# Raw pieces of the query and key projections: the copy to the high part on ScalarE alone, with all tables made anew

## The chip, the cores and the metric

The kernel runs on one core of a Trainium2 chip. The metric is the device time of one execution in microseconds. Before the change it is 384.94 us, the median of three runs (384.48 to 385.16). The names of the engines in rows are PE (TensorE), PEld (its weight load), DVE (VectorE), ACT (ScalarE), POOL (GpSimd) and SP (SyncE, which here only issues DMAs).

## The reference

Attention inside chunks of 64 tokens, then a layer of four attention experts over its output, of which each token takes the best two:

```python
def _attn_ref(q, k, v):                       # B, H, S, D = 8, 8, 576, 64
    ...                                       # q_c, k_c, v_c: nine chunks of 64 tokens
    scores = scale * np.matmul(q_c, k_c.transpose(0, 1, 2, 4, 3))
    attn = softmax(scores)                    # exp, divided by the sum + 1e-09
    out = np.matmul(attn, v_c)

def _moe_ref(x, w_gate, wq, wk, wv, wo):      # x: 8 x 576 x 512, E = 4, Hd = 64, K = 2
    logits = x @ w_gate
    topk = np.argpartition(-logits, K, axis=-1)[..., :K]
    w = softmax(logits of the two chosen)
    for e in range(E):
        q, k, v = x @ wq[e], x @ wk[e], x @ wv[e]
        scores = where(causal, -1e9, scale * (q @ k.transpose(0, 2, 1)))
        a = softmax(scores)
        ye = a @ v @ wo[e]
        out += (w of e, if e was chosen) * ye
```

All of it is in fp32. The kernel keeps that precision by splitting a factor into a high part (rounded to the type fp32r) and a low part (what is left), and by adding three matmuls for one: high by high, low by high, high by low.

## The kernel before

The 8 x 576 tokens are 36 groups of 128. `stage_a` takes one or two groups through the chunk attention (matmuls at L437, softmax on DVE, ACT and POOL, turned weights, matmuls at L504) and leaves x, high and low, in a chunk of two or three groups. Per chunk there are four query/key projections (`project_qk`, matmuls at L549, 128 x 384 in the large chunks) and per group one projection of the values and the gate (`project_v`, L409). Per batch and pair of experts there are `scores` (L671, then mask and minimum on DVE at L682, exp on ACT at L694), `weights` (scaled on POOL at L716, turned by half-turns on PE at L334, by POOL's copy at L341 with a DMA and ACT's copy at L350, and by DVE at L751), `values` (L768) and, per batch, `project_out` (L796, then a copy and the store).

A chunk of 384 tokens can reach over the end of a batch of 576. Then `project_qk` makes two parts of it. The first goes from the PSUM bank straight to the high part and the low part of the batch's queries or keys. The second belongs to the next batch, whose buffer is not yet free. It goes from the bank to a raw buffer `zr` (L554, L556, L558), which frees the bank, and later in two steps from there: a copy of `zr` to the high part (`qh` or `kh`), and the subtraction `zr` minus high part into the low part (`ql` or `kl`, L588). There are 16 such raw pieces in the program, in the batches 1, 3, 5 and 7: four of 64 columns and twelve of 192.

Nothing is scheduled at run time. `Plan.add` lists the operations. Three tables, written out in the file, say the rest: `ORDER` is the order in which all operations are emitted, and with it each engine's queue, `HOMES` gives each tile its buffer, and `SIDES` says of each operation with an `alt` whether it takes its first engine (0) or the alternative (1). Among those are all copies out of PSUM banks (ACT or DVE), the subtractions (POOL or DVE) and, before the change, the copy of a raw piece:

```python
o1 = add("ACT", act_t(n, sbuf=True), lambda f=f: f(a_copy), deps=[o1], uses=[raw, z],
         alt=("DVE", dve_t(n), lambda f=f: f(dve.tensor_copy)))        # L584, L585; runs as L583
```

The entries `w412`, `w62` and so on in `ORDER` are warm-up matmuls without use (bank, then count), all in the first 20 us. An engine works its queue strictly in order; what stands behind a waiting instruction waits too.

Of the kernel before, what the change touches and what calls it, by code (L numbers as in the profile page):

```python
# [116 lines left out]
def dve_t(n):  # L117
    return 0.075 + 1.04e-3 * n


def act_t(n, aps=0, sbuf=False):
    return (0.093 if aps or sbuf else 0.052) + 0.833e-3 * n + 0.093 * aps
# [7 lines left out]
43 63 40 109 86 66 89 w412 69 25 70 72 20 w62 46 71 73 132 47 74 49 48 75 161 50 76 51 77 112 52 10 w615 92 53 5 54 28  # L130
93 155 23 95 29 94 w03 55 96 115 57 97 78 24 116 56 98 79 80 192 99 118 w74 81 100 117 119 84 82 158 120 85 w22 101 83
# [112 lines left out]
def chunked_attention_then_attention_experts(ctx: ExitStack, tc: tile.TileContext, qt, kt, vt, wqk, wvg, wo, out):  # L244
    nc = tc.nc
    pe, dve, act, pool = nc.tensor, nc.vector, nc.scalar, nc.gpsimd
    plan = Plan()
    add = plan.add
# [282 lines left out]
    def project_qk(c, m):  # L531
# [28 lines left out]
        for k, (b, s0, n, c0) in enumerate(parts):  # L560
            z = z_s[b, pair]
# [13 lines left out]
            else:  # L575
                raw = own[k]
# [297 lines left out]
```

## Time and profile before

| | |
|---|---|
| median of three runs | 384.94 us (384.48 to 385.16) |
| the profiled execution | 383.89 us |
| its span, first to last instruction | 382.2 us |
| PE busy | 367.4 us, 96% of the span |
| DVE, ACT, POOL busy | 315.3, 282.1, 270.1 us |
| mean granted TensorE clock | 0.994 |

A busy PE is a PE whose pipelined matmuls cover the time; their ends are modelled. The time between the span and the execution's own time, 1.7 us, lies around the program. The profile is of one execution, 1.05 us faster than the median.

### The profile page before, as it was taken

The numbers are of one execution on the slowest core, as the hardware profiler recorded it, in microseconds if no ns is written. First come the engines' busy times: TensorE is split into PE (matmuls) and PEld (weight loads), VectorE is DVE, ScalarE is ACT, GpSimd is POOL, SyncE is SP. The second block draws the span as 40 slices with busy tenths as digits, with TensorE's granted clock in tenths as the row PEclk, the third lists the DMA queues.
The fourth block names the chain that finished last, engine by engine and source line by source line (L and its number), as shares of the span: only waits on it lengthen the run. The fifth ranks groups of instructions, "written<-read, shape, count | busy, mean of one in ns | idle before, by whom it ended". The sixth has DMA issues, their size and how long they took to land.

```text
span 382.2 us, 12795 instructions
## 1 busy us (share of the span) xinstructions
PE 367.4 (96%) x4876; PEld 310.3 (81%) x4876; DVE 315.3 (83%) x1040; ACT 282.1 (74%) x675; POOL 270.1 (71%) x477
## 2 busy tenths in 40 slices
PE   7999999999999999679999999999999999998996
PEld 3599989888898898577988979988798799776765
DVE  2899799899996689989986998989989588777742
ACT  1564698899796997559696687968975879998450
POOL 5546589887988459488987248979795459989700
PEclk9999999999999999989999999999999999999999
DMA  7997777989898749766665777648488303365764
GB/s 269 392 338 216 148 194 181 205 155 204 212 239 152 164 151 173 205 194 117 176 123 140 155 190 198 100 138 165 129 113 154 68 3 61 59 134 96 169 204 165
DMA packets 114221, 63.49 MB, mean 166 GB/s; under 512 B 94576, under 2 KB 94832, under 8 KB 114160
## 3 DMA queue, kind: packets, MB, share of 16 engines
q1 hardware_dynamic: 114016, 62.42, 68.5%
q8 instruction: 38, 0.62, 0.7%
q10 hardware_dynamic: 144, 0.26, 0.2%
q14 instruction: 23, 0.19, 0.2%
HBM read 30.42 MB, written 9.44 MB: 104 GB/s over the span
## 4 chain that ended last, share of the span: by engine, by line
PE 67%; DVE 15%; POOL 6%; ACT 6%; DMA 3%; issue 2%; SPq 0%; ACTq 0%; POOLq 0%; DVEq 0%
PE bank L549 19%; PE bank L409 12%; PE bank L796 11%; PE bank L768 10%; PE bank L671 7%; PE bank L437 3%; PE bank L504 3%; PE bank L334 2%; DVE at L682 2%; POOL at L716 2%; DVE mx L454 2%; DVE xl L519 2%; ACT at L694 2%; DVE kh L583 2%; POOL wp L341 2%
## 5 line engine op out<-in xcount | busy, mean ns | idle before, releaser
L694 ACT ACTIVATE at<-at,st 128x320 f32<-128x320 f32 (+4 forms) x160 | 88.3, 554 | 18.1 <-DVE st L682 17.9
L716 POOL TENSOR_SCALAR at<-at,st,gate 64x64 f32<-64x64 f32 (+4 forms) x160 | 95.6, 609 | 7.8 <-DVE st L707 5.5
L350 ACT ACTIVATE aT<-wpT 128x768 uint16<-128x768 uint16 (+1 forms) x64 | 66.3, 1055 | 5.9 <-DMA wpT<-wp 5.8
L549 PE MATMUL bank<-xh,wqk_hi 128*128 128x384 f32 (+1 forms) x208 | 68.4, 336 | 2.3 <-DVE e L449 2.3
L682 DVE CUSTOM_DVE_ANT_0 at<-bank,mask 64x64 f32<-64x64 f32 (+4 forms) x160 | 61.1, 418 | 9.2 <-PE bank L671 8.9
L341 POOL COPY wp<-at 128x768 uint16<-128x768 uint16 (+1 forms) x64 | 58.4, 930 | 13.6 <-DMA wpT<-wp 13.4
L549 PE MATMUL bank<-xh,wqk_lo 128*128 128x384 f32 (+1 forms) x208 | 66.2, 326 | 0.0
L465 POOL TENSOR_TENSOR en<-e,mx 128x512 f32<-128x512 f32 x36 | 37.2, 1044 | 24.5 <-DVE mx L456 21.5
L768 PE MATMUL bank<-aT,vv 128*64 128x448 f32 (+4 forms) x384 | 47.2, 393 | 0.8 <-DVE e L449 0.7
L768 PEld LDWEIGHTS bank<-aT,vv 128*64 128x64 f32 x384 | 25.3, 137 | 22.7 <-issue 15.3
L549 PEld LDWEIGHTS bank<-xh,wqk_hi 128*128 128x128 f32 x208 | 39.4, 189 | 4.7 <-DVE e L449 2.5
L549 PE MATMUL bank<-xl,wqk_hi 128*128 128x384 f32 (+1 forms) x208 | 42.6, 326 | 0.0
L350 ACT ACTIVATE et<-wpT 128x1024 uint16<-128x1024 uint16 x31 | 35.9, 1174 | 6.7 <-DMA wpT<-wp 6.7
L549 PEld LDWEIGHTS bank<-xh,wqk_lo 128*128 128x128 f32 x208 | 39.6, 190 | 0.2
L409 PE MATMUL bank<-wvg_hi,xh 128*128 128x260 f32 x144 | 37.8, 294 | 0.0
L751 DVE STREAM_TRANSPOSE aT<-at 32x96 f32<-32x96 f32 x128 | 34.5, 269 | 3.4 <-PE bank L768 0.7
L409 PE MATMUL bank<-wvg_lo,xh 128*128 128x260 f32 x144 | 36.1, 283 | 0.0
L549 PEld LDWEIGHTS bank<-xl,wqk_hi 128*128 128x128 f32 x208 | 35.5, 191 | 0.0
L452 ACT ACTIVATE e<-e 128x1024 f32<-128x1024 f32 (+1 forms) x21 | 19.6, 935 | 20.7 <-DVE e L449 20.5
L341 POOL COPY wp<-en 128x1024 uint16<-128x1024 uint16 x31 | 32.3, 1057 | 3.2 <-DMA wpT<-wp 3.2
L671 PE MATMUL bank<-kh,qh 64*128 64x288 f32 (+4 forms) x192 | 32.1, 331 | 0.4 <-DVE st L682 0.3
L447 DVE TENSOR_REDUCE mx<-bank 128x8 f32<-128x512 f32 (+1 forms) x42 | 24.3, 603 | 8.5 <-PE bank L437 8.3
(112 smaller groups left out, 866.4 us busy)
## 6 DMA issues: line engine op xcount, KB each, us to landing
vs<-in_vt_dram SPq DMA_DIRECT2D x36, 256.0 KB, 4.5
ks<-in_kt_dram SPq DMA_DIRECT2D x36, 256.0 KB, 3.9
qs<-in_qt_dram SPq DMA_DIRECT2D x35, 256.0 KB, 4.4
out_dram<-y SPq DMA_DIRECT2D x35, 256.0 KB, 2.3
wpT<-wp SPq DMA_TRANSPOSE x95, 3.3
at<-in_wqk_dram SPq DMA_DIRECT2D x4, 256.0 KB, 6.0
at<-in_wvg_dram SPq DMA_DIRECT2D x2, 260.0 KB, 5.3
at<-in_wo_dram SPq DMA_DIRECT2D x2, 256.0 KB, 5.3
```

The costliest lines, as they stand in the source:

```text
L341: pool.tensor_copy(p.t[:, :256 * n].rearrange("p (x n) -> p x n", x=2), src().bitcast(U16).rearrange("p (n x) -> p x n", x=2))
L350: act.activation(put().bitcast(U16).rearrange("p j (q x) -> p j q x", x=2), pt.t[:, :256 * n].rearrange("p (x j q) -> p j q x", x=2, j=n), ...
L409: pe.matmul(bk.t[0:rows, :W_VG], xp[:, k, cols], wp[:, k, :], start=(n == 0), stop=(n == 3 * KT - 1))
L465: pool.tensor_tensor(en.t.rearrange("p (s h k) -> p s h k", s=2, h=HP), ev, rv.to_broadcast([128, 2, HP, 64]), op=OP.mult)
L549: pe.matmul(bk.t[:, :width], wp[:, k], xp[:, k, 0:width], start=(n == 0), stop=(n == 3 * KT - 1))
L671: pe.matmul(bks[s].t[:rows(i), at:at + c1 - c0], q[own, cs], k[own, c0:c1], start=(x == 0), stop=(x == 2), skip_group_check=True)
L682: dve.tensor_tensor_reduce(out=a.t[:r, A_OFF[i] + c0:A_OFF[i] + c1], in0=bk.t[:r, at:at + w], in1=mask[:r, m0:m0 + w], scale=1.0, scalar=f ...
L694: act.activation(af, af, AF.Exp, scale=-1.0, bias=st.t[:r, 0, i, 0:1], accum_out=st.t[:r, 1, i, 0:1])
L716: pool.tensor_scalar(af, af, st.t[:r, 2, i, 0:1], gt.t[:r, i, e:e + 1], op0=OP.mult, op1=OP.mult)
L751: dve.transpose(dst, src)
L768: pe.matmul(bk.t[64 * s:64 * s + 64, c0 - h0:h1 - h0], vs.t[:, j, 64 * (2 * pair + s):64 * (2 * pair + s) + 64], ts[s].t[:, 448 * j + c0:4 ...
L796: pe.matmul(bk.t[:, n0:n1], up[:, k, 128 * t:128 * t + 128], wp[:, k, n0:n1], start=(n == 0), stop=(n == 5), skip_group_check=True)
```

## The change

One line of Python loses its alternative, and the three tables are other tables. The copy of a raw piece is on ACT in all 16 cases; before, `SIDES` had 7 of them on ACT and 9 on DVE.

```diff
@@ project_qk
                 def f(copy, raw=raw, z=z, cs=cs, n=n):
                     copy(z.t[hi][:, cs], raw.t[:, 0:n])
-                o1 = add("ACT", act_t(n, sbuf=True), lambda f=f: f(a_copy), deps=[o1], uses=[raw, z],
-                         alt=("DVE", dve_t(n), lambda f=f: f(dve.tensor_copy)))
+                o1 = add("ACT", act_t(n, sbuf=True), lambda f=f: f(a_copy), deps=[o1], uses=[raw, z])
@@ ORDER (first line; all others differ too, and there is one line more)
-43 63 40 109 86 66 89 w412 69 25 70 72 20 w62 46 71 73 132 47 74 49 48 75 161 50 76 51 77 112 52 10 w615 92 53 5 54 28
+63 43 40 25 135 109 86 w49 69 70 72 66 71 73 20 w45 46 74 132 28 49 75 50 112 29 155 47 76 48 77 51 10 52 5 w616 78 53
...
@@ HOMES, SIDES: other digits throughout
```

Because `ORDER` is one text line longer, lines of the changed kernel above the edit have numbers one higher (L450 for L449, L312 for L311); from L586 on they are the same, since the edit takes one line away.

The multiset of the other instructions is the same but for sides. Of the copies out of PSUM, 18 of turned weights (`aT`) and 4 of `et` go from ACT to DVE; 8 of `uh`, 5 of `y` and 2 of `vv` go from DVE to ACT; among `xh`, `qh`, `kh` and `zr` some change places both ways. Of the subtractions of raw pieces 9 of 16 are on DVE in both. Of the eight subtractions of weights, DVE has one of `wqk` and two of `wo` before, and one of `wqk` and one of `wvg` after. The warm-up matmuls are 34 instead of 38.

On DVE, in the second half of the scores of batch 2 (experts 2 and 3), this is what stands around a raw piece of batch 3's keys before the change (`zr` is the raw piece, `kh` and `kl` its high and low part, `mx` and `e` the maximum and the exponents of the chunk attention; `ISA` is the masked minimum of L682):

```order
L519 TENSOR_TENSOR xl1_96<-bank2_63,xh1_94 128x2x128
L449 TENSOR_TENSOR e0_81<-bank0_61,mx2_91 128x8x64
L751 STREAM_TRANSPOSE aT0_115<-at1_112 32x3x32 x4
L583 CAST kh1_106<-zr0_97 128x192
L447 TENSOR_REDUCE mx2_91<-bank6_67 128x8
L588 TENSOR_TENSOR kl1_108<-zr0_97,kh1_106 128x192
L449 TENSOR_TENSOR e0_81<-bank6_67,mx2_91 128x8x64
L682 ISA at0_111,st0_123<-bank4_65,mask_145 128x288
```

On DVE the same piece (and its query twin) now leaves only the subtraction:

```order
L682 ISA at2_113,st1_124<-bank6_67,mask_145,st1_124 128x288
L682 ISA st1_124 128x1
L588 TENSOR_TENSOR ql0_103<-zr2_99,qh0_101 128x192
L801 COPY y0_127<-bank7_68 128x512
L682 ISA at0_111,st0_123<-bank5_66,mask_145 128x320
L682 ISA st0_123 128x1
L588 TENSOR_TENSOR kl0_107<-zr0_97,kh0_105 128x192
L801 COPY y2_129<-bank2_63 128x512
```

The cast is gone from DVE's queue, and the chunk attention's subtraction at L449 no longer stands behind one.

On ACT, these are the rows of the queue in the same stretch before the change, with no raw piece among them (`at` are the exps of the scores, `vv` and `y` copies out of banks):

```order
L694 ACTIVATE at2_113,st1_124<-at2_113,st1_124 128x448
L311 ACTIVATE y0_127<-bank5_66 128x512
L311 ACTIVATE y1_128<-bank1_62 128x512
L350 ACTIVATE aT1_116<-wpT2_122 128x3x256
L694 ACTIVATE at2_113,st1_124<-at2_113,st1_124 64x64
L311 ACTIVATE y2_129<-bank0_61 128x512
L452 ACTIVATE e0_81<-e0_81 128x16x64
```

On ACT the two pieces now stand between the exps of these scores:

```order
L453 ACTIVATE e0_81<-e0_81 128x16x64
L555 ACTIVATE kh1_106<-bank1_62 128x384
L312 ACTIVATE vv1_110<-bank3_64 64x260 x2
L694 ACTIVATE at0_111,st0_123<-at0_111,st0_123 128x192
L312 ACTIVATE qh0_101<-zr2_99 128x192
L312 ACTIVATE kh0_105<-zr0_97 128x192
L694 ACTIVATE at0_111,st0_123<-at0_111,st0_123 128x576
L694 ACTIVATE at2_113,st1_124<-at2_113,st1_124 128x192
```

Each of the two waits until PE has read the buffer that it writes, and the exps behind them wait with them.

At the start of the program SP issued its loads in this order (`ks` and `qs` are keys and queries of a group, `vs` its values, `at` here the landing place of weights):

```order
L327 DMA vs0_77<-in_vt_dram 128x512
L323 DMA ks0_73<-in_kt_dram 128x512
L324 DMA qs0_69<-in_qt_dram 128x512
L323 DMA ks1_74<-in_kt_dram 128x512
L323 DMA ks2_75<-in_kt_dram 128x512
```

Now it issues them so:

```order
L324 DMA ks0_73<-in_kt_dram 128x512
L325 DMA qs0_69<-in_qt_dram 128x512
L328 DMA vs0_77<-in_vt_dram 128x512
L324 DMA ks1_74<-in_kt_dram 128x512
L384 DMA at0_111<-in_wvg_dram 128x520
```

The first group's keys and queries come ahead of its neighbour's values, and half of the value weights comes ahead of the third group.

## Rows read from the trace of the kernel before

**Rows 1.** The page: busy time, share of the span and instructions of each engine.
```profile
PE 367.4 (96%) x4876; PEld 310.3 (81%) x4876; DVE 315.3 (83%) x1040; ACT 282.1 (74%) x675; POOL 270.1 (71%) x477
```

**Rows 2.** Timeline, PE: start, us, line, tiles, count, idle before and releaser.
```profile
156.74 0.44 PE L549 MATMUL bank<-xh,wqk_hi 128*128 128x384 f32 x1 [2.26 <-DVE e L449]
...
159.04 0.71 PE L334 MATMUL bank<-ident,at 64*128 64x64 f32 x16
...
160.62 1.09 PE L504 MATMUL bank<-et,vs 64*64 64x64 f32 x58 [0.60 <-DVE kl L573]
...
164.40 1.15 PE L437 MATMUL bank<-ks,qs 64*64 64x64 f32 x60 [2.61 <-DVE ql L570]
...
165.48 0.44 PE L549 MATMUL bank<-xh,wqk_hi 128*128 128x384 f32 x1
...
169.06 0.42 PE L409 MATMUL bank<-wvg_hi,xh 128*128 128x260 f32 x1
```

**Rows 3.** Timeline, DVE, the same stretch.
```profile
149.71 5.51 DVE L583 CAST kh<-zr 128x192 fp32r<-128x192 f32 x1
...
156.01 0.68 DVE L449 TENSOR_TENSOR e<-bank,mx 128x512 f32<-128x512 f32 x1
...
161.92 1.70 DVE L583 CAST qh<-zr 128x192 fp32r<-128x192 f32 x1
```

**Rows 4.** Timeline, POOL, the same stretch.
```profile
149.69 2.04 POOL L465 TENSOR_TENSOR en<-e,mx 128x512 f32<-128x512 f32 x2
151.73 1.42 POOL L716 TENSOR_SCALAR at<-at,st,gate 128x320 f32<-128x320 f32 x2
153.09 1.03 POOL L341 COPY wp<-en 128x1024 uint16<-128x1024 uint16 x1
154.07 1.04 POOL L341 COPY wp<-at 128x1024 uint16<-128x1024 uint16 x1
155.10 0.39 POOL L716 TENSOR_SCALAR at<-at,st,gate 64x64 f32<-64x64 f32 x1
160.84 3.07 POOL L716 TENSOR_SCALAR at<-at,st,gate 128x448 f32<-128x448 f32 x5 [5.35 <-DVE st L707]
```

**Rows 5.** Stretches: us, busy (x) of PE, PEld, DVE, ACT, POOL, granted clock, DMA.
```profile
166.00:169.40 3.40, 3.40 (x13) 3.40 (x12) 3.40 (x6) 0.92 (x3) 3.40 (x5) 0.50 0.80 270
```

**Rows 6.** Line L583: count, min/median/max ns, first and last start, forms.
```profile
L583 DVE CAST kh<-zr x6: 243/274/5514, 49.9 to 308.5; 128x192 fp32r<-128x192 f32 x5, 128x64 fp32r<-128x64 f32 x1
L583 DVE CAST qh<-zr x3: 177/306/1701, 53.0 to 161.9; 128x192 fp32r<-128x192 f32 x2, 128x64 fp32r<-128x64 f32 x1
```

**Rows 7.** Timeline, POOL and DVE, near 230 us.
```profile
229.11 2.16 POOL L341 COPY wp<-en 128x1024 uint16<-128x1024 uint16 x2
...
229.89 0.47 DVE L588 TENSOR_TENSOR ql<-zr,qh 128x192 fp32r<-128x192 f32 x1
230.28 1.09 DVE L583 CAST kh<-zr 128x192 fp32r<-128x192 f32 x1
```

**Rows 8.** Line L390, the subtractions of weights.
```profile
L390 DVE TENSOR_TENSOR wo_lo<-at,wo_hi x2: 678/1001/1324, 26.9 to 35.0; 128x512 fp32r<-128x512 f32 x2
```

**Rows 9.** Groups by shape, ACT: busy us, mean ns, idle before.
```profile
L311 ACT ACTIVATE qh<-zr 128x192 fp32r<-128x192 f32 x4 | 1.4, 361 | 0.0
```

**Rows 10.** Timeline, PE, near 349 us.
```profile
348.89 0.47 PE L334 MATMUL bank<-ident,at 64*128 64x64 f32 x8 [1.27 <-POOL at L716]
349.28 0.50 PE L796 MATMUL bank<-wo_hi,uh 128*128 128x512 f32 x1
349.62 0.40 PE L796 MATMUL bank<-wo_lo,uh 128*128 128x512 f32 x1
349.85 0.40 PE L796 MATMUL bank<-wo_hi,uh 128*128 128x512 f32 x1
```

**Rows 11.** Timeline, SP and PE, the first microseconds.
```profile
1.74 0.42 SPq L324 DMA_DIRECT2D qs<-in_qt_dram  x1
...
1.25 4.88 PE L834 MATMUL bank<-warm 128*128 128x512 bf16 x12 [1.25 <-DVE warm L281]
```

More of the change, by code (lines that the diff above doesn't have):

```diff
@@ L129 @@
 ORDER = """
-43 63 40 109 86 66 89 w412 69 25 70 72 20 w62 46 71 73 132 47 74 49 48 75 161 50 76 51 77 112 52 10 w615 92 53 5 54 28
-93 155 23 95 29 94 w03 55 96 115 57 97 78 24 116 56 98 79 80 192 99 118 w74 81 100 117 119 84 82 158 120 85 w22 101 83
[82 rows of a table removed]
+63 43 40 25 135 109 86 w49 69 70 72 66 71 73 20 w45 46 74 132 28 49 75 50 112 29 155 47 76 48 77 51 10 52 5 w616 78 53
+115 80 79 54 23 118 161 116 24 w32 92 119 117 81 95 120 93 55 84 96 89 56 121 82 57 192 94 122 58 83 97 123 85 98 0 59
+61 60 w52 138 13 99 62 124 100 139 158 8 757 141 198 140 14 142 125 15 143 126 101 35 758 144 9 127 102 30 103 167 128
[82 rows of a table added]
@@ L214 @@
 """
 HOMES = """
-2103110231111672300010100002345332450212765412230113033275002010010363633111004111211010063022200340020322100037100322
-0321311220211450111222671112110100671220113370010220311140012233013131110226700001112400101103002412200022502020011003
-5333112060202001122430221003431100221311711221003161301001222763300024311112202002603330016200100003115110021130702021
-2110171221000060003201201170332641310013070260710162140151143001057002112574201000057221173314212336342610122110200221
-4727002611124506472156510200217645031011113700220135611233751046102211422200064000526172505025042420630710310511300211
@@ L221 @@
-2335361520111000422002737710021734273010011122211760501705030651412411213327635401000224311110554730021462610102200031
-1221702415240512250040610201025103173311106233127651340122112400115107732100166521012020211201160540723031343440316112
-3334342501012021122036327300212124631012202512013003522050015171450451217017176006105301512331725421012125320012762650
-02124643001122053200101101162223264014471531332014017012001350112534753012074474701122053120112065040327111
+2103110231111457600020100004532332011313270312236702025061001140000764511022145111100021132033300262021322000002111033
@@ new lines @@
+3741302001111030002223731102121120351331000070000121301010031100413001013222501133322000002213107211110027402021211205
+2330221461100011322020111330450202011122611222111061300011322373302225311132200012102211134700020111106710022235602110
+0022117330001200001211012210112531303215300230511030673111563112014002167350201202064211215432032131537151020015112012
+1713122001167464376247012520012071460101016320124557531233621740100110150122202701701210011114007331616513206220300033
+3126134471001104010226743052100765264100122751010655342615032316631213733124251211001102610224123152100167260011001402
@@ L225 @@
+2222114221230715031040726314141107002204005713320573420122107011011463162100721630010221531200410401706211376252014513
+3210352701121234002156643601201704501000120300214243015221123001230756111374157067000205733126151200112000621002143460
+12010735201121202210071213022426137754561203312164302012112602100755776200105570601001260002112407161105230
 """
 SIDES = """
-0010001100010110000000000001000010110010000000111110100010001011000000111001100010111110011000001100100010100010001001
-1010111010010011110111001001100100100111011100100100111000110100100011111101111010010000111110011110000010111110110011
@@ L229 @@
-0111101001101010001001110100011011011010110101010111110000100011001101001101001101101000100110110011000001110010011011
-111101101111111101010111100
+0001010000000100010111011011000000110000110000100010111000101101001110000010111010111110100111111010011111101100100100
+1011111110001111111001111100110110101011000110110000001101100110000100110110101101000101110010001001110011001110001100
+1101111010100001011000101110011111111011011001001000110100001101101110111011101011110010110111110001111110011110111000
@@ L231 @@
+01000000000
 """
```

164 rows, old and new, of the table ORDER are left out of this document.

## The prediction

> **What bounds the kernel now.** I read the page's busy times first. TensorE is covered for 367.4 of 382.2 us [rows 1], so the time is its own work plus 14.8 us of idle time, and DVE, ACT and POOL matter only where TensorE waits for them. Then I read the waits of PE, and its timeline where they are long. Three of the waits lie within 10 us, at 156.74, 160.62 and 164.40: 2.26 + 0.60 + 2.61 = 5.47 us, all for DVE [rows 2]. The largest other wait behind the start is 1.27 us [rows 10]. The reader is to see that this one place is the only one of its size.
>
> The cause is on DVE in the same stretch: the copy of a raw piece, 128 x 192 out of SBUF into SBUF, starts at 149.71 and takes 5.51 us [rows 3]. The line's median is 274 ns [rows 6]. POOL works without a gap from 149.69 to 155.10 + 0.39 [rows 4], and DVE goes on just as that burst ends, at 155.22. A second copy takes 1.70 us at 161.92, inside a burst that starts at 160.84 and lasts 3.07 us [rows 3, 4]; a third takes 1.09 us at 230.28 and ends (231.37) when two POOL copies end (231.27) [rows 7]. The six others found no such burst. So a copy on DVE that reads and writes SBUF waits until POOL pauses. L449, two places behind the long copy, frees a bank for TensorE; it starts at 156.01, and TensorE starts at 156.74.
>
> A rule stands close to this. The Trainium skill's page "SBUF — State Buffer", section "Who interferes with whom", says that DVE in its two-port mode and GpSimd take a shared pair of ports as an exclusive lock, held for one whole instruction, and that the later one blocks until the first has finished. By that, the copy would wait for one POOL instruction, 1.04 us at most here [rows 4], which DVE could make good (3.0 us of slack, below), and the change would gain nothing at this place. The trace disagrees: one copy waited out a whole burst of seven instructions. I go by the rows.
>
> After the third wait the granted clock is 0.50 for 3.4 us [rows 5], the lower of the two levels, 1.2 GHz; TensorE had been idle for 5.47 of the 11 us before it fell.
>
> **The change part by part.**
>
> The nine copies leave DVE. The long one with its median of 0.27 us would end 5.24 us earlier, L449 would end at 156.01 + 0.68 − 5.24 = 151.45, and TensorE wants its bank at 156.74 − 2.26 = 154.48: it is 3.0 us early, and the first wait goes. The third wait is for the low part of the queries, which stands on DVE right behind the second held copy; with 1.43 and the backlog of 5.24 us gone it goes too. The 0.60 us are a wait for the low part of keys that TensorE itself had computed just before (bank out, high part, low part, bank free), and I leave them in. Gain 2.26 + 2.61 = 4.87 us; ends 2.26 (the first alone) and 5.47. What is late next at this place is that 0.60.
>
> The clock. Twelve matmuls of one projection took 169.06 − 165.48 = 3.58 us at the low level and 159.04 − 156.74 = 2.30 at the full one [rows 2]. Without the stall I count the difference as gained, 1.28 us; ends 0 (it falls elsewhere) and 1.28.
>
> The copies arrive on ACT: nine at 361 ns [rows 9] are 3.2 us, beside 100 us in which ACT is idle (382.2 − 282.1, [rows 1]). ScalarE's seven copies before the change include no long one (four of 192 columns have a mean of 361 ns, and no idle time before them). Cost 0, hidden by TensorE's own work; if that cover is missing, a copy costs what it takes, 3.2 us in all. The wait that it adds: nine of the sixteen wait for PE to have read the buffer they write, and behind them stand exps of the scores, which POOL and then TensorE wait for. That is a rival below.
>
> The other sides that change (18 and 4 copies to DVE, 15 to ACT) leave both engines under TensorE's load: DVE idles 67 us, ACT 100 [rows 1]. Cost 0; if a bank comes free late because of one, the price is a wait like the largest other one, 1.27 us [rows 10]. The nine subtractions on DVE stay nine.
>
> The written order. In the old order TensorE changes between its four shapes of matmul (128 x 128, 64 x 128, 128 x 64, 64 x 64) 141 times, in the new one 134 times, counted in the order of both. One change costs, at 349.28, the first step of 0.34 us instead of 0.23 [rows 10], so 0.11 us. Seven fewer are 0.8 us; ends 0 (hidden in a wait) and 0.8.
>
> The start. The first group's queries are issued one load earlier, 1.74 becoming some 1.3 us [rows 11], a gain of one issue, about 0.4. Against it DVE gets the low part of half the value weights as its ninth instruction, 0.68 us [rows 8], ahead of the chain that the first turned weights wait for, and it waits there for a load. The four warm-up matmuls less are 4 x 4.88 / 12 = 1.6 us at most [rows 11]; they fill time in which TensorE waits for loads, so I count nothing for them. The start is 0 in the sum; ends −2.0 and +0.7. In the end of the program both orders hold back the same thirteen output projections to fill the last two weight chains; 0.
>
> Sum: 4.87 + 1.28 + 0.8 = 7.0 us. The span becomes 375.2, the execution 376.9 with the 1.7 us around it. The profiled execution was 1.05 us below the median, so the median to expect is 377.9 us.
>
> **Rivals.**
>
> Slower: ACT's queue stops at the raw pieces. Five pairs of pieces of 192 columns now stand side by side in ACT's queue, each behind a wait for PE (the one shown for batch 3 among them), and each stops the exps behind it. For it: before, only two of seven on ACT waited for PE. Against it: the four in the row showed no idle time [rows 9]. Priced by the longest wait that TensorE showed, 2.61 us [rows 2], it outweighs the gain from three pairs on; with four it is 377.9 + 10.4 = 388.3 us. Chance 0.11.
>
> Given back: another order has other waits. For it: the order is new throughout, and a wait like the 0.60 us [rows 2] comes of order alone. Against it: the old order's largest wait of its own is 1.27 us [rows 10]. Three such waits make 381.7 us. Chance 0.16.
>
> The burst holds the subtractions instead. Two inputs in SBUF, on DVE, now beside the burst of POOL's weights in batch 2. For it: L390 took 1324 ns once instead of 678 [rows 8]. Against it: at 229.89 one of 192 columns took 0.47 us in the middle of POOL's copies, where the copy of the same width behind it took 1.09 us and waited for their end [rows 7]. The stall of 4.87 + 1.28 would be back: 384.1 us. Chance 0.05.
> The same page and section speak for this rival: an instruction of DVE with two SBUF inputs contends with a GpSimd instruction that reads SBUF. The trace agrees with some price (0.65 us at L390), not with a full block.
>
> The change doesn't remove what the median holds: the long copy was an accident of the profiled execution. Against it: that execution was the fastest shown (383.89 against 384.48 to 385.16). Time 384.1 us, chance 0.03.
>
> **How the numbers follow.** The forecast holds 0.65. Its own range: 2.3 to 5.5 for the stall, 0 to 1.3 for the clock, 0 to 0.8 for the shapes and −2.0 to +0.7 for the start, which do not all fall on one side, give 375 to 381 us. The range for 8 in 10 takes in the order's rival and the edge of the two at 384.1, and at the low end one more of the old waits gone and a good start: 373.5 to 384.0. A difference under 0.2%, 0.8 us, can't be told from none here. Faster than 384.2: 0.65, nearly all of 0.16 and 0.03 of the two cases at 384.1, so 0.83. Slower than 385.7: 0.11. The same: 0.06.
>
> **What the next profile would show.** No DVE instruction in its table that copies `zr`, and no DVE instruction outside the start far over its group's mean; PE's waits for `e` at L450 and `ql` at L571 of over 2 us gone; a mean clock near 1.0 with no fall before the end; sixteen copies of `zr` on ACT with means near 0.36 us. Wrong would be: a subtraction at L588 of over 1 us on DVE, ACT idle for PE at the raw copies, or new PE waits that sum to over 8 us behind the start.

## The result

The changed kernel takes 380.05 us (median of four, 378.66 to 380.55) beside 384.71 us for the kernel before (384.24 to 385.16): ratio 0.9873, 95% interval 0.9844 to 0.9902, a gain of 4.7 us where 7.0 were forecast. The profiled execution took 380.55 us, its span is 378.8. The two profiled executions, 383.89 and 380.55, lie 3.3 us apart, less than the medians; what is read from profiles below accounts for these two.

The page of the kernel after, busy times; the kernel before is in [rows 1]:
```profile
PE 364.5 (96%) x4872; PEld 309.4 (82%) x4872; DVE 312.4 (82%) x1043; ACT 285.7 (75%) x672; POOL 270.3 (71%) x477
```
TensorE's busy time fell by 2.9 us, its idle time from 14.8 to 378.8 − 364.5 = 14.3. That is odd for a change that was to take away waits of 4.87 us. The timeline of PE says why; three new waits stand there, 1.18 + 2.36 + 2.55 = 6.09 us, where [rows 2] had 5.47:
```profile
159.74 0.50 PE L796 MATMUL bank<-wo_hi,uh 128*128 128x512 f32 x1 [1.18 <-DVE ql L571]
...
163.76 0.59 PE L410 MATMUL bank<-wvg_hi,xh 128*128 128x260 f32 x1 [2.36 <-ACT aT L312]
...
321.62 0.39 PE L410 MATMUL bank<-wvg_hi,xh 128*128 128x260 f32 x1 [2.55 <-DVE kl L574]
```
The copies are as forecast: none on DVE, sixteen on ACT with medians of 348 ns ([rows 9] had a mean of 361). Line L312, count, min/median/max ns, first and last start:
```profile
L312 ACT ACTIVATE qh<-zr x8: 240/348/356, 45.1 to 311.6; 128x192 fp32r<-128x192 f32 x6, 128x64 fp32r<-128x64 f32 x2
L312 ACT ACTIVATE kh<-zr x8: 240/348/366, 52.3 to 311.3; 128x192 fp32r<-128x192 f32 x6, 128x64 fp32r<-128x64 f32 x2
```
But the instruction behind the copy, the subtraction at L588 that makes the low part, is now held in its place. Line L588 on DVE, first in the kernel before, then after:
```profile
L588 DVE TENSOR_TENSOR ql<-zr,qh x5: 227/343/469, 73.1 to 309.5; 128x192 fp32r<-128x192 f32 x4, 128x64 fp32r<-128x64 f32 x1
L588 DVE TENSOR_TENSOR kl<-zr,kh x4: 342/350/389, 137.7 to 309.2; 128x192 fp32r<-128x192 f32 x4
```
```profile
L588 DVE TENSOR_TENSOR ql<-zr,qh x5: 185/346/2354, 46.2 to 314.7; 128x192 fp32r<-128x192 f32 x3, 128x64 fp32r<-128x64 f32 x2
L588 DVE TENSOR_TENSOR kl<-zr,kh x5: 437/1011/3383, 52.9 to 312.2; 128x192 fp32r<-128x192 f32 x4, 128x64 fp32r<-128x64 f32 x1
```
Four took over 1.3 us, two in batch 3 and two in batch 7. Timeline of DVE and of POOL beside the first two:
```profile
150.87 1.58 DVE L588 TENSOR_TENSOR ql<-zr,qh 128x192 fp32r<-128x192 f32 x1
...
153.38 3.38 DVE L588 TENSOR_TENSOR kl<-zr,kh 128x192 fp32r<-128x192 f32 x1
156.69 0.68 DVE L801 COPY y<-bank 128x512 f32<-128x512 f32 x1
```
```profile
151.83 1.80 POOL L716 TENSOR_SCALAR at<-at,st,gate 64x64 f32<-64x64 f32 x3
153.57 1.80 POOL L342 COPY wp<-at 128x768 uint16<-128x768 uint16 x2
155.36 1.19 POOL L716 TENSOR_SCALAR at<-at,st,gate 128x448 f32<-128x448 f32 x2
```
The longer one goes on when POOL's burst ends (155.36 + 1.19 = 156.55), the shorter one inside the burst; the burst is POOL's work on the weights of batch 2. Behind it waits DVE's copy of an output block (L801, 156.69), and behind that a queue. Timeline of SP's queue, then of ACT:
```profile
153.23 4.50 SPq L807 DMA_DIRECT2D out_dram<-y  x2
157.90 3.68 SPq L346 DMA_TRANSPOSE wpT<-wp  x2
```
```profile
162.32 0.94 ACT L351 ACTIVATE aT<-wpT 128x768 uint16<-128x768 uint16 x1 [4.86 <-DMA wpT<-wp]
```
SP stood at the store of that block until 157.73 and issued the turning transfer of weights behind it, which ACT waited for, 4.86 us; TensorE's 2.36 us at 163.76 are a wait for ACT behind that. So, by the trace, the held subtractions stand at the head of two waits on TensorE, one of them by way of SP's queue, which never touches the pieces.

The clock fell once more after those waits (columns as in [rows 5], 0.51 is the lower level, 1.2 GHz):
```profile
163.60:167.10 3.50, 3.34 (x16) 3.11 (x18) 1.29 (x2) 3.16 (x9) 3.50 (x5) 0.51 0.43 111
```
What did improve is TensorE's work itself and the start. Groups of the warm-up matmuls, before and after:
```profile
L834 PE MATMUL bank<-warm 128*128 128x512 bf16 x38 | 11.4, 448 | 1.2 <-DVE warm L281 1.2
```
```profile
L834 PE MATMUL bank<-warm 128*128 128x512 bf16 x34 | 10.2, 448 | 1.2 <-DVE warm L282 1.2
```
Busy less warm-ups is 367.4 − 11.4 = 356.0 before and 364.5 − 10.2 = 354.3 after. So the span's 3.4 us are 1.7 of work, 1.2 of warm-ups and 0.5 of idle time. Each of the two sums of work holds one stretch at the lower clock.

### The profile page after: what moved, and what is told of

Its sections match the earlier page's. It is cut to its first block, busy times and chain, and to the rows that moved or that the text cites. A ratio compares the mean times of both kernels' runs of the same rounds, so it can differ in the third digit from the quotient of the medians.

```text
span 378.8 us, 12784 instructions
## 1 busy us (share of the span) xinstructions
PE 364.5 (96%) x4872; PEld 309.4 (82%) x4872; DVE 312.4 (82%) x1043; ACT 285.7 (75%) x672; POOL 270.3 (71%) x477
## 4 chain that ended last, share of the span: by engine, by line
PE 75%; DMA 8%; DVE 7%; POOL 4%; ACT 4%; issue 2%; SPq 0%; ACTq 0%; POOLq 0%
PE bank L550 20%; PE bank L796 13%; PE bank L410 12%; PE bank L768 11%; PE bank L671 8%; DMA wpT<-wp 4%; PE bank L438 4%; PE bank L505 4%; PE bank L335 2%; DVE at L682 2%; DMA at<-in_wvg_dram 2%; ACT at L694 2%; POOL wp L342 1%; DMA ks<-in_kt_dram 1%; DVE kl L588 1%
## 5 line engine op out<-in xcount | busy, mean ns | idle before, releaser
L694 ACT ACTIVATE at<-at,st 128x576 f32<-128x576 f32 (+4 forms) x160 | 88.3, 554 | 11.8 <-DVE st L682 10.7
L351 ACT ACTIVATE aT<-wpT 128x1024 uint16<-128x1024 uint16 (+1 forms) x64 | 66.5, 1056 | 11.4 <-DMA wpT<-wp 11.1
L550 PE MATMUL bank<-xh,wqk_hi 128*128 128x384 f32 (+1 forms) x208 | 67.0, 329 | 0.0
L342 POOL COPY wp<-at 128x1024 uint16<-128x1024 uint16 (+1 forms) x64 | 58.1, 928 | 10.4 <-DMA wpT<-wp 10.3
L682 DVE CUSTOM_DVE_ANT_0 at<-bank,mask 128x448 f32<-128x448 f32 (+4 forms) x160 | 60.5, 421 | 5.0 <-PE bank L671 4.9
L466 POOL TENSOR_TENSOR en<-e,mx 128x512 f32<-128x512 f32 x36 | 37.6, 1056 | 14.3 <-DVE mx L457 12.9
L410 PE MATMUL bank<-wvg_hi,xh 128*128 128x260 f32 x144 | 38.8, 300 | 4.9 <-DVE kl L574 2.5
L410 PEld LDWEIGHTS bank<-wvg_hi,xh 128*128 128x128 f32 x144 | 27.6, 192 | 7.8 <-ACT aT L312 2.8
L796 PE MATMUL bank<-wo_hi,uh 128*128 128x512 f32 (+1 forms) x74 | 29.9, 406 | 1.2 <-DVE ql L571 1.2
```

What stands on the lines that cost most here:

```text
L342: pool.tensor_copy(p.t[:, :256 * n].rearrange("p (x n) -> p x n", x=2), src().bitcast(U16).rearrange("p (n x) -> p x n", x=2))
L351: act.activation(put().bitcast(U16).rearrange("p j (q x) -> p j q x", x=2), pt.t[:, :256 * n].rearrange("p (x j q) -> p j q x", x=2, j=n), ...
L410: pe.matmul(bk.t[0:rows, :W_VG], xp[:, k, cols], wp[:, k, :], start=(n == 0), stop=(n == 3 * KT - 1))
L466: pool.tensor_tensor(en.t.rearrange("p (s h k) -> p s h k", s=2, h=HP), ev, rv.to_broadcast([128, 2, HP, 64]), op=OP.mult)
L550: pe.matmul(bk.t[:, :width], wp[:, k], xp[:, k, 0:width], start=(n == 0), stop=(n == 3 * KT - 1))
L682: dve.tensor_tensor_reduce(out=a.t[:r, A_OFF[i] + c0:A_OFF[i] + c1], in0=bk.t[:r, at:at + w], in1=mask[:r, m0:m0 + w], scale=1.0, scalar=f ...
```

## The experiments

Theory A: what cost the time is that DVE's work from SBUF to SBUF is held while POOL runs a burst; theory B: the new order made the gain, and the holds are a side matter. Ratios are to the kernel before on the same chip, with 95% intervals.

**The copies alone, old order.**
```diff
-o1 = add("ACT", ..., uses=[raw, z], alt=("DVE", ...))
+o1 = add("ACT", ..., uses=[raw, z])          # its digit of SIDES is skipped
```


> The kernel before with its nine raw copies moved from DVE to ACT, and nothing else: old written order, old buffers, all other sides as they were. Theory A (a DVE copy from SBUF to SBUF is held until POOL pauses, and that is what was slow): the waits of 2.26 and 2.61 us at 156.74 and 164.40 go and the clock stays up there, 384.7 - 4.9 - 1.3 = 378.6 us; if the subtraction behind each copy is now held in its place, 381 to 384. Theory B (the gain of 4.7 us comes of the new order: start, fewer shape changes, other waits): 384.7, no change.


Measured 0.9947 (0.9925 to 0.9969), 382.75 us. Timeline of DVE and waits of PE:
```profile
151.05 4.64 DVE L588 TENSOR_TENSOR kl<-zr,kh 128x192 fp32r<-128x192 f32 x1
```
```profile
156.35 0.44 PE L549 MATMUL bank<-xh,wqk_hi 128*128 128x384 f32 x1 [1.83 <-DVE e L449]
160.24 1.09 PE L504 MATMUL bank<-et,vs 64*64 64x64 f32 x58 [0.62 <-DVE kl L573]
162.53 0.69 PE L437 MATMUL bank<-ks,qs 64*64 64x64 f32 x31 [1.12 <-DVE ql L570]
```
The copy is gone and the subtraction behind it waits in the same burst: 4.64 us in place of 5.51. Moving the copy alone buys 2 us, which is theory A's second case (381 to 384); B's 384.7 lies outside the runs' interval.

**The copies back on DVE, new order.**
```diff
+if (b, m) in ((1, 1), (1, 3), (3, 0), (3, 1), (3, 2), (3, 3), (5, 2), (5, 3), (7, 2)):
+    o1 = add("DVE", dve_t(n), lambda f=f: f(dve.tensor_copy), deps=[o1], uses=[raw, z])
```


> The changed kernel with the nine copies that DVE had before put back on DVE, in the new written order. Theory A: the pairs at 150 and 312 us stand beside POOL's bursts, so copies are held there for 1 to 5 us, besides the subtractions: 382 to 387 us. Theory B: the order carries the gain, 380.05 within 0.8 us.


Measured 0.9896 (0.9862 to 0.9929), 381.04 us: not told apart from the changed kernel. B's range is missed by 0.2 us and A's by 1.0. Lines L584 (copies) and L591 (subtractions), the longest of each:
```profile
L584 DVE CAST kh<-zr x6: 245/355/1665, 61.6 to 299.0; 128x192 fp32r<-128x192 f32 x5, 128x64 fp32r<-128x64 f32 x1
L591 DVE TENSOR_TENSOR ql<-zr,qh x5: 183/345/2949, 45.8 to 313.8; 128x192 fp32r<-128x192 f32 x3, 128x64 fp32r<-128x64 f32 x2
L591 DVE TENSOR_TENSOR kl<-zr,kh x5: 356/733/1667, 52.5 to 311.9; 128x192 fp32r<-128x192 f32 x4, 128x64 fp32r<-128x64 f32 x1
```
Whichever comes into the burst waits; with the subtractions held anyway, the copies add little: 0.9896 − 0.9873 = 0.0023, or 0.9 us, which the intervals don't tell from none. So a gain of the edited line by itself is not shown in the new order.

**Four subtractions to POOL.**
```diff
+def low_alt(b, m, n, f):
+    if (b, m) in ((3, 1), (3, 3), (7, 1), (7, 3)):
+        return "Pool", 0.19 + 2.07e-3 * n, lambda f=f: f(pool)
+    return "DVE", dve_t(n), lambda f=f: f(dve)
```


> The changed kernel with four low parts (keys and queries of the second pair in batches 3 and 7, the ones that took 1.58, 3.38, 1.33 and 2.35 us on DVE) made by POOL instead, in place. Theory A: PE's waits of 1.18 us at 159.74 and 2.55 us at 321.62 go or shrink under 0.8; POOL gets 4 x 0.60 us more: 376.5 to 378 us. Rival C (those waits are of the order: banks and turned weights late by DMA): 380 us; if POOL's longer bursts decide, 381 to 382.


Measured 0.9705 (0.9678 to 0.9733), 373.3 us, below even theory A's figure. The page, and the warm-ups' group:
```profile
PE 361.9 (97%) x4869; PEld 307.4 (83%) x4872; DVE 304.2 (82%) x1039; ACT 285.0 (77%) x672; POOL 272.1 (73%) x481
```
```profile
L839 PE MATMUL bank<-warm 128*128 128x512 bf16 x31 | 9.4, 453 | 1.6 <-DVE warm L282 1.2 <-issue 0.3
```
All three waits are gone, the one behind SP's queue too; the longest wait left behind the start is 0.65 us, and the clock stays up (mean 0.999). I had priced two of the three waits and left out the clock. This version beats both kernels.

**All low parts to POOL**, in the changed kernel (`add("Pool", ...)` without the choice of DVE).


> The changed kernel with all sixteen low parts of raw pieces on POOL, so that DVE has neither copy nor subtraction of them. Theory A: the six others were held for 0.7 us at most and hid nothing on TensorE's path: 373.3 within 1 us. Rival (POOL's load): 375 to 377 us.


Measured 0.9733 (0.969 to 0.9776), 375.40 us on a chip where the kernel before takes 386.36: no better than four; the intervals overlap.

**Old order, copies on ACT and low parts on POOL** (the first edit and this last one in the kernel before).


> The kernel before, in its old order, with its nine copies moved to ACT and its nine low parts of raw pieces to POOL. Theory A (the hold was all that was wrong at 150 to 165 us; with copies alone moved, a subtraction of 4.64 us took its place): PE's waits of 1.83 and 1.13 us there go, 382.75 - 1.8 - 1.1 - 1.3 = 378.5 us. Theory B (the new order brings most, and holds are a side matter): 382 us or more.


Measured 0.9836 (0.9795 to 0.9876), or −6.3 us (4.8 to 7.9). The page, and the warm-ups' group:
```profile
PE 365.7 (97%) x4874; PEld 309.3 (82%) x4876; DVE 305.0 (81%) x1022; ACT 284.1 (75%) x684; POOL 273.8 (73%) x486
```
```profile
L834 PE MATMUL bank<-warm 128*128 128x512 bf16 x36 | 10.8, 443 | 1.5 <-DVE warm L281 1.2 <-issue 0.2
```
In the old order the holds cost 6.3 us. Free of holds, the new order is still ahead: by 0.9836 − 0.9733 = 0.0103, or 4.0 us, with all low parts on POOL in both (two runs on one chip), and by 0.0131, or 5.0 us, against the run with four. So both theories have a part: the holds cost about 6 us in either order, and the order gives 4 to 5. The two profiled spans shown lie further apart, 377.3 − 371.6 = 5.7 us; of these, work is (365.7 − 10.8) − (361.9 − 9.4) = 2.4, and the rest is warm-ups and idle time.

**Is it POOL? Short scalings in batches 2 and 6.**
```diff
-af = a.t[:r, o_:o_ + n]
+af = a.t[:r, o_:o_ + (8 if b in (2, 6) else n)]
```


> The changed kernel, subtractions on DVE as they are; in batches 2 and 6 POOL scales only the first 8 columns of each block of weights instead of 64 to 576, so the bursts beside the held subtractions lose most of their length (the weights of these batches stay unscaled). Theory A (POOL's burst holds them): of the four subtractions over 1.3 us none stays over 1.3, PE's waits at 159.74 and 321.62 go: 373 to 376 us. Rival (something else holds DVE there, the burst is only beside it): subtractions of 1.3 to 3.4 us stay, 379 to 380 us.


Measured 0.9671 (0.9629 to 0.9713), 372.17 us. L588 on DVE:
```profile
L588 DVE TENSOR_TENSOR ql<-zr,qh x5: 184/345/354, 45.7 to 307.4; 128x192 fp32r<-128x192 f32 x3, 128x64 fp32r<-128x64 f32 x2
L588 DVE TENSOR_TENSOR kl<-zr,kh x5: 346/440/1052, 52.7 to 305.9; 128x192 fp32r<-128x192 f32 x4, 128x64 fp32r<-128x64 f32 x1
```
The four take 0.35 us each (the 1052 ns is in batch 5, beside a burst that was not shortened). DVE's code and order are untouched, so POOL's burst is the cause. One of the four came into a pause of POOL; the other three came 0.16 us or less into a POOL instruction and went first, and that instruction took 0.2 to 0.3 us longer than its like.

**Gaps in the bursts**, first put in the wrong place.
```diff
 pool.tensor_scalar(af, af, ...)
+if b in (3, 7):
+    pool.tensor_copy(pad[:r], af[:, n - 1:n])
```


> The changed kernel, subtractions on DVE as they are; in batches 3 and 7 a one-column copy of each scaled block follows its scaling on POOL and reads what that wrote, so that POOL waits a little between the two. Theory A2: no subtraction on DVE over 1.1 us (1.58, 3.38, 1.33 and 2.35 before); POOL has 40 instructions more of some 0.15 us; PE's waits at 159.74 and 321.62 shrink: 375 to 378 us. Rival L or chance: the holds stay, and the longer bursts make 381 to 384 us.


Measured 0.9975 (0.9932 to 1.0017), with subtractions of 1.55, 2.92 and 2.95 us. That tells nothing on gaps: the bursts beside the subtractions of batch 3 are the weights of batch 2, and of batch 7 those of batch 6. With `b in (2, 6)`:


> The edit of the run with gaps in POOL's bursts, now in batches 2 and 6, whose weights are those beside the held subtractions (in batches 3 and 7 it came after them): a one-column copy of each scaled block follows its scaling. Theory A2 (gaps let DVE in): no subtraction of the four over 1.1 us, 376 to 379 us. Rival L2 (gaps don't matter: DVE takes one of POOL's instruction ends by chance, gap or none): one or more of 1.3 to 3.4 us stays, 380 to 384 us.


Measured 0.9883 (0.9848 to 0.9917). L589, the subtractions, and a wait of PE:
```profile
L589 DVE TENSOR_TENSOR ql<-zr,qh x5: 188/345/732, 46.0 to 314.9; 128x192 fp32r<-128x192 f32 x3, 128x64 fp32r<-128x64 f32 x2
L589 DVE TENSOR_TENSOR kl<-zr,kh x5: 346/601/1031, 52.6 to 313.4; 128x192 fp32r<-128x192 f32 x4, 128x64 fp32r<-128x64 f32 x1
```
```profile
183.39 0.24 PE L672 MATMUL bank<-kh,qh 64*64 64x64 f32 x1 [3.27 <-DVE aT L740]
```
The holds are gone (1.03 us at most), as A2 had it; the time isn't: POOL has more to do (278.4 us busy for 270.3), and a wait of 3.27 us opened at 183.39. So A2's time was wrong. Its mechanism is not shown either: the two of the four that took 1.03 and 0.73 us went on at ends of POOL instructions (152.34 and 315.41) behind which the next one followed without a gap.

**Bursts by themselves.** Four kernels without the attention; DVE comes into a POOL burst with a copy (`zh<-zr`) or a subtraction (`zl<-zr,zh`) of 192 columns, or a copy out of a bank.

> No attention at all: bursts of POOL (none; 7 weight scalings of 448; 5 repackings of 1024 uint16; 5 normalisations of 512; 3 scalings and 3 repackings by turns), each beside two DVE instructions of one kind that start 0.7 us into it: a copy of 192 columns SBUF to SBUF, a subtraction of two SBUF inputs, or a copy out of a PSUM bank. The output is zeros. Theory A: the bank copy takes its idle time (0.3 us) everywhere, the copy and the subtraction take the rest of the burst (about 2.5 to 4 us) for the first one, 0.3 us for the second. A lock held for one POOL instruction: no more than one POOL instruction, 0.5 to 1.05 us, each. Theory B: all 0.3 us.


The instructions were put in another order than I had written, so the groups mixed and DVE met each burst near its start; nothing took over 1.1 us. With the order held:

> No attention at all: bursts of POOL, each beside two DVE instructions of one kind that start about 0.8 us into it (copy SBUF to SBUF, subtraction of two SBUF inputs, copy out of a bank; 192 columns each). The output is zeros. The bursts: none; 7 scalings of 448 columns on the same columns (each waits for the one before it, which leaves gaps); 7 scalings on separate columns; 4 repackings of 1024 uint16 into separate buffers; 3 scalings and 3 repackings by turns. Theory A2 (POOL keeps DVE out as long as its next instruction follows without a gap): beside the gapless bursts the first copy or subtraction takes 2 to 4 us in most cases, beside the burst with gaps at most 0.9 us; the bank copy 0.35 everywhere. Rival L (a lock for one instruction): at most one POOL instruction, 0.55 to 1.05 us, plus its own time, in every burst.


Lines L89 (copy), L90 (subtraction), L91 (out of a bank):
```profile
L89 DVE CAST zh<-zr x20: 244/568/977, 10.5 to 187.9; 128x192 fp32r<-128x192 f32 x20
L90 DVE TENSOR_TENSOR zl<-zr,zh x20: 348/659/1074, 16.0 to 195.1; 128x192 fp32r<-128x192 f32 x20
L91 DVE CAST zl<-bank x20: 346/352/358, 20.3 to 202.0; 128x192 fp32r<-128x192 f32 x20
```
A bank's copy is never held. Of the 32 others that met a burst, four came behind a gap, 0.04 to 0.14 us into the next POOL instruction, and took their usual time, and 28 waited for the end of the running POOL instruction and no longer, gap or none: rival L was right here, A2 wrong.

> No attention: POOL bursts of 14 instructions (scalings of 64 to 512 columns on separate columns, repackings of 768 and 1024 into separate buffers, without a gap), and DVE comes with a copy or a subtraction of 192 columns six times in each, between two reductions that it does alone. The first four bursts with ScalarE, TensorE and the DMA queues idle, the last four beside 60 matmuls, 16 exps and 4 turning transfers. The output is zeros. Rival L (one instruction, always): none over 1.3 us, early or late, quiet or not. Theory D (a request that comes while POOL's queue is long is passed over at some of POOL's instruction ends): from the second one on, several of 1.5 to 4 us in the quiet bursts too. Theory E (other traffic makes DVE miss its turn): 1.5 to 4 us only in the last four bursts.


None of 48 took over 0.82 us, early or late, quiet or beside other work; D and E fell.

> No attention: bursts of 18 POOL instructions made closer to the kernel's own than in the runs before: blocks of 64 partitions among those of 128, scalars from tiles that ScalarE wrote, repackings that read the block scaled just before, normalisations with a broadcast factor. DVE comes with its copy or subtraction of 192 columns seven times in each, right behind copies out of a PSUM bank, as in the kernel. The first four bursts quiet, the last four beside matmuls, exps and turning transfers. The output is zeros. Rival L (always the next instruction end): none over 1.3 us. Theory F (one of these kinds of POOL instruction passes the turn on to the next): some of 1.5 us or more, at the same places of the burst in every repetition. If neither shows in any burst, why the kernel's DVE misses several ends stays open.


Now the hold is there, and rival L fell. Lines L114 (copy) and L115 (subtraction); then the first burst, DVE and POOL:
```profile
L114 DVE CAST zh<-zr x28: 249/250/6624, 11.5 to 181.3; 128x192 fp32r<-128x192 f32 x28
```
```profile
L115 DVE TENSOR_TENSOR zl<-zr,zh x28: 348/348/6720, 35.7 to 206.4; 128x192 fp32r<-128x192 f32 x28
```
```profile
11.48 4.06 DVE L114 CAST zh<-zr 128x192 fp32r<-128x192 f32 x1
...
16.62 6.62 DVE L114 CAST zh<-zr 128x192 fp32r<-128x192 f32 x1
```
```profile
12.40 2.03 POOL L108 TENSOR_TENSOR en<-ev,one 128x512 f32<-128x512 f32 x2
14.39 1.03 POOL L104 COPY wp<-at 128x1024 uint16<-128x1024 uint16 x1
15.41 1.66 POOL L101 TENSOR_SCALAR at<-at,st,gt 64x64 f32<-64x64 f32 x3
17.03 1.80 POOL L104 COPY wp<-at 128x768 uint16<-128x768 uint16 x2
18.81 1.19 POOL L101 TENSOR_SCALAR at<-at,st,gt 128x448 f32<-128x448 f32 x2
19.97 1.03 POOL L108 TENSOR_TENSOR en<-ev,one 128x512 f32<-128x512 f32 x1
21.00 0.39 POOL L101 TENSOR_SCALAR at<-at,st,gt 64x64 f32<-64x64 f32 x1
21.33 1.80 POOL L104 COPY wp<-at 128x768 uint16<-128x768 uint16 x2
```
In each of the eight bursts two DVE instructions came inside it, and all sixteen were held, 4.1 to 4.5 us and 6.6 to 6.7 us, quiet or not, at the same places of the burst each time, as theory F had it. The first goes on inside the burst, at the end of the fifth POOL instruction that it meets (14.39 + 1.03 = 15.42; two scalings stand ahead of the rows shown). The second comes 0.15 us into its POOL instruction and goes on only when the burst ends (23.13). This burst differs from the one before it in four ways at once: blocks of 64 partitions, repackings that read what was just scaled, normalisations, and DVE coming from bank copies rather than reductions. Which of them lets POOL keep its turn is open.

## Why the prediction was right in sign and wrong in its working

- **The cause.** Right: the copies waited for POOL's burst, and it is the burst (short scalings: 0.35 us). "Until POOL pauses" and "a whole burst of seven instructions" were too strong for the rows themselves. The long copy ended at 155.22, 0.11 us after the end of POOL's sixth instruction (154.07 + 1.04), with the seventh running until 155.49; the second copy ended at 161.92 + 1.70 = 163.62, inside a burst that lasted at least until 163.91 [rows 3, 4].
- **What the stall is worth.** Right in size: 4.87 + 1.28 = 6.15 forecast, 6.3 measured in the old order free of holds. But this needs the subtractions out of DVE as well as the copies; the copies alone gave 2.0.
- **"The nine subtractions on DVE stay nine", cost 0.** This is the step that failed. They became ten (five of queries and five of keys, above), which matters little; four of them now stand beside bursts, and taking these off DVE is worth 380.05 − 373.3 = 6.8 us (by ratios 0.9873 − 0.9705 = 0.0168, 6.5 us). It is the third rival, priced at 6.15 and given 0.05. Its place was batch 2's burst, as written, and also batch 6's. The argument against it was one row, 0.47 us beside POOL's copies [rows 7]: one turn that DVE got, at the end of the POOL instruction that ran when it came, read as a rule. The row for it, 1324 ns at L390 [rows 8], was the better witness.
- **The clock.** The 1.28 us were given back: 0.51 at 163.6 to 167.1, behind the new waits. In the four profiled executions without the long holds there is no such fall (mean clock 0.999 to 1.0), though two of the six runs in the old order free of holds show 0.995.
- **The order, 0.8 us.** Far too small: together with the start, 4.0 to 5.0 us free of holds. The work fell by 1.7 us (2.4 free of holds), where seven shape changes at 0.11 were counted. Counted by matmul in the two traces, without the warm-ups, the shape changes 155 times before and 153 after, which makes 0.2 us at that price; so the price or the reason is another, and which was not tried.
- **The start, 0 (−2.0 to +0.7).** Outside these bounds. The first matmul on loaded data moved from 6.99 to 5.42 us, the first value projection from 19.79 to 18.82 (with 32 small matmuls fewer ahead of it), and the four warm-ups that I counted at nothing left 1.2 us of the span, since the idle time did not grow in their place. Timelines of PE, before and then after:
```profile
6.99 0.70 PE L437 MATMUL bank<-ks,qs 64*64 64x64 f32 x32 [0.86 <-DMA qs<-in_qt_dram]
...
19.79 0.39 PE L409 MATMUL bank<-wvg_hi,xh 128*128 128x260 f32 x1
```
```profile
5.42 0.87 PE L438 MATMUL bank<-ks,qs 64*64 64x64 f32 x21 [0.15 <-DMA qs<-in_qt_dram]
...
18.82 0.39 PE L410 MATMUL bank<-wvg_hi,xh 128*128 128x260 f32 x1
```
- **The copies on ACT, cost 0.** Right; the rival of a stopped queue did not come (ACT's longest idle time before one of the sixteen is 0.15 us). The rival of other waits did not come either: all three new long ones go with the holds.

So two errors of opposite sign, some 4 us of order and start not counted (4.0 to 5.0 less the 0.8) and 6.5 us of held subtractions not believed, left the sum 2.3 us off. That the time fell inside the range is luck: what the copies were to gain was taken back by the subtractions, and the gain that was measured came with the order. Of the signs I had named as wrong, a subtraction of over 1 us did appear; and the fall of the clock, which was not to come, came.

## What to carry to other kernels

When an instruction is late because of a neighbour, moving that one instruction moves the wait to the next of its kind in the queue: move all that read or write in the same way. Gaps in the neighbour's burst went with shorter holds here, but gained no time. A single quick case beside a burst shows that a turn can be had, not that it always is. And a hold is paid for in other queues: look at what stands behind the held engine's stores.

## What the runs showed of the hardware

Beside POOL's scalings, repackings and normalisations, a DVE copy from SBUF to SBUF, or a subtraction of two SBUF inputs, mostly has to wait; a DVE copy of 192 columns out of a bank does not (346 to 358 ns in every burst of the second small kernel). The wait ends with one POOL instruction in three of the small kernels (1.1 us at most), but with the fifth or the ninth in the last (4.06 and 6.62 us) and with the sixth in the kernel before (5.51 us). Almost every hold of over 1 us ends 0.11 to 0.15 us after the end of some POOL instruction for a copy, and 0.20 to 0.23 us for a subtraction, often with the next POOL instruction already begun (0.31 and 0.37 us in two cases); which end it is, the runs don't explain.

It can also go the other way. In the kernel before, a copy that came 0.18 us into one of POOL's small instructions for the gates took its usual time. Timelines of POOL and DVE:
```profile
308.34 0.54 POOL L614 TENSOR_SCALAR gw<-gw 128x80 f32<-128x80 f32 x1
```
```profile
308.52 0.26 DVE L583 CAST kh<-zr 128x192 fp32r<-128x192 f32 x1
```
L614 takes 0.43 us in six of its eight runs in that trace; with this copy it took 0.54.

The Trainium skill's page "SBUF — State Buffer", section "Who interferes with whom", says that a DVE instruction with two SBUF inputs contends with a GpSimd instruction that reads SBUF, and a DVE copy in its two-port mode with GpSimd too; whoever issues first holds the shared ports for its whole instruction, and the other is blocked. On who contends, the runs here agree (bank copies in 346 to 358 ns, the others held); on how long, the measurements above decide against one instruction as a bound.
